# The down product of five blocks in seven products over pairs of inner tiles, with the weights' combinations kept in DRAM

## The chip, the cores and the metric

The kernel runs on one core of one Trainium2 chip. The metric is the device time of one execution in microseconds (us). A core has five engines that run side by side and wait for each other through semaphores: PE (TensorE, matrix products; PEld are its weight loads), DVE (VectorE), ACT (ScalarE), POOL (GpSimd) and SP (SyncE), which issues almost all transfers between DRAM and the on-chip memory SBUF. Matrix products land in PSUM, which has eight banks of 512 float32 columns on 128 partitions.

## What is computed

Two layers, each a Fourier mixing (A) and a gated product (B), on x of 2048 rows and 640 columns:

```python
def _A_ref(x, dft_seq_re, dft_seq_im, dft_hid_re, dft_hid_im):
    a = jnp.einsum("bsd,ed->bse", x, dft_hid_re)
    b = jnp.einsum("bsd,ed->bse", x, dft_hid_im)
    return jnp.einsum("ts,bse->bte", dft_seq_re, a) - jnp.einsum("ts,bse->bte", dft_seq_im, b)

def _B_ref(x, w_gate, w_up, w_down):
    g = jnp.einsum("bsd,df->bsf", x, w_gate)
    u = jnp.einsum("bsd,df->bsf", x, w_up)
    return jnp.einsum("bsf,fd->bsd", _sigmoid(g) * u, w_down)

x = x + _A_ref(_layernorm(x), ...)
x = x + _B_ref(_layernorm(x), ...)
x = x + _A_ref(_layernorm(x), ...)
x = x + _B_ref(_layernorm(x), ...)
```

The inner width F is 1728: 13 tiles of 128 and a tail of 64. Everything is float32, and the kernel keeps that precision by splitting each operand into a high and a low float16 part; one product is then three matmul passes (high x high, high x low, low x high).

## The kernel before

x stays in SBUF (`X`, 16 groups of 128 rows). The Fourier mixing uses the symmetry of the matrices (folded rows), so the kernel also tests that the matrices have it: `load_rows`/`test_rows` and `load_cols`/`test_cols` read parts of the DFT matrices in layer 0 and 1 into two buffers in turn (SP), compare them (DVE, lines 1295 to 1298 and 1312 to 1315) and add the squares (ACT, line 1273). Weights are tested for their size too (`absmax`, line 229). If a test fails, a general path follows; it is not entered with these inputs.

The gated product goes in four blocks of 512 rows per layer (`block[b]`). A block has a gate and up part and a down part.

- Gate and up, block 0 of a layer: `gate_up` takes one inner tile per step, three passes each over five 128-row pieces of x, 512 columns wide (PE line 1047), into two banks per tile. `gated_parts` then splits the result into high and low parts for the down product (lines 1071 and 1072).
- Gate and up, blocks 1 to 3: `seven` takes two inner tiles per double step in a form with seven products of half blocks (PE line 1093, 256 columns wide; the tail tile on line 1176). The weights' combinations for it (`S`, 512 KB per tile) are made in layer 0 and kept in DRAM, and `load_s` brings G, S and U of a tile back for each block. `snap` copies a running sum from PSUM to SBUF (ACT, line 1097), after which the same bank goes on accumulating. `part_three` adds (DVE, 1129 and 1130), `gate` applies the sigmoid (ACT, 1139), `up` multiplies (DVE, 1149 and 1151), `up_parts` splits (ACT 1160, DVE 1161). A double step holds four banks, and the chains of the two tiles before hold two more until `up`.
- Down: `down` has two steps for each of four row groups. It multiplies 13 inner tiles in three passes and the tail in two with both 320-column halves of the weights (PE line 1240), one bank per half, and adds the two banks to `X` (DVE line 1255).

All work is written out in one order by hand. `steps` lists the products; `at(u, f, ...)` puts a job at place u among the steps, so that it is issued before that step's matmuls, and in a double step of `seven` at one of four places. Each engine runs its own instructions strictly in the order of issue, SP's transfers too. While a block's down part runs, the next block is normalised (`pair_stats`, `pair_scale`, `pair_apply`, `pair_combine`, `pair_parts`, DVE, ACT and POOL) and turned round by transposing transfers (`pair_transpose`, SP line 512), and its first weights are loaded.

Memory in SBUF is dealt out by `Slots`: 388 units of 128 float32 columns, of which 218 are fixed. A freed place is taken again by a later tile, whose first writer then waits for the last reader.

At the layer change the last rows of layer 0 are folded (`fold_stats`, `fold_power`, `fold_scale`, `fold_rows`, `fold_join`) while PE works through products of the Fourier mixing (`sequence`, line 771, and `hidden`, line 853). The reciprocal root of the variance (`rstd_power`, `rstd_step`, lines 396 to 407) runs on POOL in small instructions; `fold_scale` adds lines 602 to 607. The first layer's opening has the same work in an order of its own (`OPENING`).

## Time and profile before

| | |
|---|---|
| Time, median of 3 runs | 1177.77 us (1177.05 to 1178.28) |
| The profiled execution: its own time | 1176.77 us |
| its span, first to last instruction | 1174.6 us |
| mean granted TensorE clock | 0.985 |
| PE matmuls in all | 8784 |
| down matmuls (line 1240) | 2624, eight blocks of 328 |
| gate and up part of a block 1 to 3 | 80.5 to 80.8 us |
| down part of a block | 44.5 to 44.6 us |
| DMA moved | 216.41 MB, mean 184 GB/s |

How to read the profile: a group line gives source line, engine, operation, output <- input with partitions x elements and type, count | busy us, mean ns of one | idle time of the engine just before these instructions and what ended it. The chain of waits follows the last instruction back to whatever released it. A line of the view by stretch gives the stretch, its length, then busy us and (count) of PE, PEld, DVE, ACT and POOL, the granted clock, the busy share of the 16 DMA engines, and GB/s. A line in the order of time gives start, length, engine, line and operation; idle time before it stands in brackets with what ended it. "SPq" is SP's queue of transfers: the length is the issue, not the landing.

### The profile page before, as it was taken

To read this page: it belongs to the slowest core of one execution; us is meant where nothing else is said; L and a number is where in the kernel's file an instruction comes from. 1 tells how busy PE (TensorE), PEld (TensorE's weight loads), DVE (VectorE), ACT (ScalarE), POOL (GpSimd) and SP (SyncE) were. 2 spreads that over 40 slices of the span, in tenths; PEclk is the share of its full clock that TensorE was granted. 3 is DMA by queue.
4 is the path that set the end of the run, shared out by engine and by line. 5 is a ranking of instruction groups with operands and counts; after the bars stand their busy time and mean duration, and the time that the engine had idled before them with its cause. 6 is when DMAs were issued, how large, how long until landed. Compare 5 with 4: busy or idle time off the path is not lost.

```text
span 1174.6 us, 22659 instructions
## 1 busy us (share of the span) xinstructions
PE 1135.1 (97%) x8784; PEld 861.1 (73%) x8784; DVE 731.8 (62%) x1571; ACT 503.7 (43%) x1078; POOL 170.5 (15%) x365
## 2 busy tenths in 40 slices
PE   5699999999999999999999999999999999999997
PEld 2367445788878887888776744678887888788874
DVE  8694998768656776676326476746975457524530
ACT  5665475245524653365303422415552455225420
POOL 3414565210102010100011101000000001000000
PEclk9699999999999999999999999999999999999999
DMA  9353797859595969779301642687959773767301
GB/s 277 124 154 95 251 337 269 229 176 261 168 215 168 262 176 225 218 228 251 83 15 58 242 134 62 192 233 227 249 159 241 234 253 94 178 199 255 120 19 38
DMA packets 225622, 216.41 MB, mean 184 GB/s; under 512 B 68034, under 2 KB 181851, under 8 KB 225502
## 3 DMA queue, kind: packets, MB, share of 16 engines
q1 hardware_dynamic: 224862, 212.23, 61.9%
q0 software_dynamic: 640, 2.62, 0.6%
q8 instruction: 71, 1.16, 0.4%
q14 instruction: 49, 0.40, 0.1%
HBM read 171.03 MB, written 30.40 MB: 171 GB/s over the span
## 4 chain that ended last, share of the span: by engine, by line
PE 86%; issue 4%; POOL 3%; DMA 2%; DVE 2%; ACT 2%; SPq 0%; POOLq 0%; DVEq 0%; ACTq 0%
PE acc L1093 36%; PE acc L1240 30%; PE acc L1047 12%; PE acc L771 2%; PE acc L853 2%; PE acc L1176 2%; DMA kept_o<-big 1%; DVE big L238 1%; DMA big<-kept_w 1%; POOL quad L397 0%; DMA big<-in_ct 0%; DVE big L662 0%; SPq L1289 0%; POOL big L998 0%; PE acc L778 0%
## 5 line engine op out<-in xcount | busy, mean ns | idle before, releaser
L1093 PE MATMUL acc<-big 128*128 128x256 f16 x4212 | 462.9, 273 | 0.1
L1093 PEld LDWEIGHTS <-big 128*128 128x128 f16 x4212 | 411.6, 98 | 49.0 <-DMA big<-kept_w 0.4
L1240 PE MATMUL acc<-big 128*128 128x320 f16 x2624 | 357.7, 299 | 0.0
L1240 PEld LDWEIGHTS <-big 128*128 128x128 f16 x2624 | 256.4, 98 | 100.0
L1097 ACT ACTIVATE big<-acc 128x256 f32<-128x256 f32 x312 | 116.5, 381 | 193.8 <-PE acc L1093 189.0
L1047 PE MATMUL acc<-big 128*128 128x512 f16 (+1 forms) x990 | 176.6, 341 | 3.8 <-ACT big L527 1.7
L1047 PEld LDWEIGHTS <-big 128*128 128x128 f16 x990 | 96.3, 98 | 83.3 <-ACT big L236 2.6
L1273 ACT ACTIVATE big<-big 128x768 f32<-128x768 f32 (+8 forms) x104 | 79.5, 764 | 132.5 <-DVE big L1298 96.4
L1161 DVE TENSOR_TENSOR big<-big 128x512 f16<-128x512 f32 x78 | 53.8, 690 | 110.0 <-ACT big L1160 110.0
L1255 DVE SCALAR_TENSOR_TENSOR big<-acc,big 128x320 f32<-128x320 f32 x64 | 28.4, 484 | 82.8 <-PE acc L1240 82.7
L238 DVE SCALAR_TENSOR_TENSOR big<-big 128x640 f16<-128x640 f32 (+6 forms) x81 | 62.9, 815 | 4.7 <-ACT big L236 4.7
L1139 ACT ACTIVATE big<-big 128x512 f32<-128x512 f32 x78 | 47.9, 627 | 38.2 <-DVE big L1130 37.3
L1295 DVE TENSOR_TENSOR big<-big 128x256 f32<-128x256 f32 x64 | 26.7, 416 | 55.5 <-DMA big<-in_ct 55.5
L236 ACT ACTIVATE big<-big 128x640 f16<-128x640 f32 (+6 forms) x81 | 49.7, 665 | 14.3 <-DMA big<-big 8.8
L1130 DVE TENSOR_TENSOR big<-big,acc 128x512 f32<-128x512 f32 x78 | 53.2, 682 | 4.1 <-PE acc L1093 3.9
L771 PE MATMUL acc<-big 128*128 128x256 f16 (+5 forms) x288 | 44.0, 315 | 11.7 <-ACT big L657 9.7
L1149 DVE SCALAR_TENSOR_TENSOR big<-acc,big 128x256 f32<-128x256 f32 x78 | 32.6, 418 | 34.4 <-PE acc L1093 30.1
L1160 ACT ACTIVATE big<-big 128x512 f16<-128x512 f32 x78 | 48.8, 625 | 6.5 <-DVE big L1151 5.6
L771 PEld LDWEIGHTS <-big 128*128 128x128 f16 (+1 forms) x288 | 31.8, 116 | 24.6 <-ACT big L657 12.5
L853 PE MATMUL acc<-big 128*128 128x321 f16 (+3 forms) x324 | 49.2, 304 | 0.0
L505 ACT ACTIVATE big<-big 128x384 f16<-128x384 f32 (+2 forms) x48 | 28.9, 647 | 34.6 <-DVE big L487 22.6
L853 PEld LDWEIGHTS <-big 128*128 128x128 f16 (+3 forms) x324 | 28.8, 96 | 19.2 <-issue 7.5
(169 smaller groups left out, 975.2 us busy)
## 6 DMA issues: line engine op xcount, KB each, us to landing
big<-kept_w SPq DMA_DIRECT2D x125, 320.0 KB
big<-kept_s SPq DMA_DIRECT2D x75, 512.0 KB
big<-in_ct SPq DMA_DIRECT2D x256, 128.0 KB
big<-kept_w SPq DMA_DIRECT2D x78, 192.0 KB
kept_w<-big SPq DMA_DIRECT2D x41, 320.0 KB
big<-in_ct SPq DMA_DIRECT2D x32, 256.0 KB
kept_s<-big SPq DMA_DIRECT2D x13, 512.0 KB
big<-in_wg SPq DMA_DIRECT2D x16, 320.0 KB
```

The costliest lines, as they stand in the source:

```text
L236: nc.scalar.activation(dh, src, AF.Copy, scale=s)
L238: nc.vector.scalar_tensor_tensor(dl, src, s, dh, op0=OP.mult, op1=OP.subtract)
L771: nc.tensor.matmul(o, xv[:, 384 * xp + c0 : 384 * xp + c0 + n], moving(r, cps[cp]), start=(i % 2 == 0 and r == 0 and xp == HI and cp == HI ...
L853: nc.tensor.matmul(ps[:m, :EC], z[:, at : at + m], w[:, 384 * wp : 384 * wp + EC], start=(d == 0 and zp == HI and wp == HI), stop=(d == ND ...
L1047: nc.tensor.matmul(ps, w[wp][:, d * P : (d + 1) * P], xt[:, xp, :], start=(d == 0 and wp == HI and xp == HI), stop=(d == ND - 1 and wp == LO))
L1093: nc.tensor.matmul(ps, wt, xt, start=start and n == 0, stop=n == len(todo) - 1, skip_group_check=not start)
L1097: nc.scalar.activation(dst, ps, AF.Copy)
L1130: nc.vector.tensor_tensor(v, v, other, op=OP.add)
L1160: nc.scalar.activation(s.parts[HI], v, AF.Copy)
L1161: nc.vector.tensor_tensor(s.parts[LO], v, s.parts[HI], op=OP.subtract)
L1240: nc.tensor.matmul(held["pd", e][0][:, :EH], held["ht", j].parts[hp][:, i * P : (i + 1) * P], held["w", 2, j].parts[wp][:, e * EH : (e + 1 ...
L1273: nc.scalar.activation(v, v, AF.Square, accum_out=new_sum()[:p])
```

## The change

Layer 0's block 2 and all four blocks of layer 1 (`PAIRED`) get another down part, `down_pairs`. Twelve inner tiles form six pairs; the rows of a block form two halves of two row groups, the 640 output columns two halves of 320. Each pair's 2 x 2 product of halves is made with seven products in place of eight, and sums over the pairs stay in PSUM: product n over all six pairs is one run of 18 matmuls per row group, 23 where the thirteenth tile and the tail are added (`REST`). Four banks per row group (a to d) are read by DVE twice each into `X`, in part while the bank goes on accumulating: bank a takes products 1, 6, 7 and the leftover 8, and is read after each.

The left sides are made beside the gate and up part: `first_parts`, `second_parts` and `sum_parts` take the place of the plain splits. The right sides are the weights and four combinations of them, T1 to T4. They are made once in layer 0, blocks 1 and 2 (`load_raw`, `make_t`, `split_t`, `keep_t`), kept in DRAM, and T2 to T4 are loaded for each paired block (`load_t`, 18 transfers of 160 KB), T2 and T3 into the place of the block's turned-round rows. The scales DS and PH change with it, and half of the even tiles' weights is tested from a separate load (`load_others`, `test_others`).

In paired blocks G, S and U are loaded separately and later, and `Slots` deals out places in fours below a limit, with the left sides at the top. The matrix tests no longer start between place 12.5 of a block and 4.5 before the next. In layer 1 the joins of hidden groups 2 and 3 move into block 0. `rstd` of the folds and of the first normalisation runs on DVE but for the power itself; a factor 2 is folded in; `fold_join` is issued in three rounds over both halves; evictions at the layer change come one or two places earlier; a folded row is kept in DRAM between blocks 2 and 3.

```diff
-DS = 2.0**11
+DS = 2.0**9
...
-PH = 2.0**-16
+PH = 2.0**-18
...
+NP = 6
+PAIRED = (2,), (0, 1, 2, 3)
...
-    def rstd_step(t, n, to):
+    def rstd_step(t, n, to, on=nc.gpsimd, times=-1.0):
         c = [t[:, :n, k] for k in range(24)]
-        nc.gpsimd.tensor_tensor(c[16], c[14], c[15], op=OP.mult)
...
+        on.tensor_tensor(c[16], c[14], c[15], op=OP.mult)
+        on.tensor_tensor(c[17], c[16], c[15], op=OP.mult)
+        on.tensor_scalar(c[18], c[17], -0.5 * to, 1.5 * to, op0=OP.mult, op1=OP.add)
+        on.tensor_tensor(c[19], c[18], c[15], op=OP.mult)
+        if on is nc.vector:
+            on.scalar_tensor_tensor(c[20], c[12], times, c[19], op0=OP.mult, op1=OP.mult)
...
-    def load_s(j):
-        nc.sync.dma_start(take(5, "G", j).f16, kept["w", 0, j])
...
+    def load_s(j, do="GSU"):
+        if "G" in do:
+            v = take(8, "GU", j).f32
...
+    def gated_parts(j, paired=False):
+        if paired and j < 2 * NP:
+            if j % 2 == 0:
+                first_parts(j // 2, held["hf", j].f32)
+            else:
+                second_parts(j // 2, held["hf", j - 1].f32, held["hf", j].f32)
+                sum_parts(j // 2)
...
+    def first_parts(p, v):
+        a = both(take(6, "A", p, top=UNITS - 8 * NP), 768)[:, :, :256]
+        f = take(8, "af", p).f32
+        nc.vector.tensor_tensor(f[:, 512:768], v[:, :256], v[:, 256:], op=OP.subtract)
+        nc.scalar.activation(a[:, 0], v[:, :256], AF.Copy)
+        nc.vector.tensor_tensor(a[:, 1], v[:, :256], a[:, 0], op=OP.subtract)
+
+    def second_parts(p, v, w):
+        a, f = both(held["A", p], 768)[:, :, 256:], held["af", p].f32
+        s1, s2, s4 = (f[:, 256 * n : 256 * (n + 1)] for n in (0, 1, 3))
+        nc.scalar.activation(a[:, 0], w, AF.Copy)
+        nc.vector.tensor_tensor(s1, v[:, 256:], w[:, 256:], op=OP.add)
+        nc.vector.tensor_tensor(s2, s1, v[:, :256], op=OP.subtract)
+        nc.vector.tensor_tensor(s4, w[:, :256], s2, op=OP.subtract)
+        nc.vector.tensor_tensor(a[:, 1], w, a[:, 0], op=OP.subtract)
+
+    def sum_parts(p):
+        f, s = held["af", p].f32, both(take(8, "AS", p, top=UNITS), 1024)
+        for c in (slice(0, 512), slice(512, 1024)):
+            nc.scalar.activation(s[:, 0, c], f[:, c], AF.Copy)
+        for c in (slice(0, 512), slice(512, 1024)):
+            nc.vector.tensor_tensor(s[:, 1, c], f[:, c], s[:, 0, c], op=OP.subtract)
+        drop("af", p)
...
+    def make_t(p):
+        v, w = (held["dr", 2 * p + k].f32 for k in range(2))
+        b11, b12, b21, b22 = v[:, :EH], v[:, EH:], w[:, :EH], w[:, EH:]
+        nc.vector.tensor_tensor(b11, b12, b11, op=OP.subtract)
+        nc.vector.tensor_tensor(b12, b22, b12, op=OP.subtract)
+        nc.vector.tensor_tensor(b22, b22, b11, op=OP.subtract)
+        nc.vector.tensor_tensor(b21, b21, b22, op=OP.subtract)
...
+    LEFT = {1: ("A", 0), 2: ("A", 1), 4: ("A", 2), 5: ("AS", 0), 6: ("AS", 1), 7: ("AS", 2), 3: ("AS", 3)}
+    CHAIN = {1: "a", 2: "c", 5: "b", 3: "b", 4: "d", 6: "a", 7: "a", 8: "a"}
+    READ = {1: (0, 0), 2: (0, 0), 5: (1, 1), 3: (0, 1), 4: (1, 0), 6: (0, 1), 7: (1, 0), 8: (1, 1)}
+    REST = (2, 3, 4, 8)
...
+    def down_pairs(b, todo, store):
...
+        def mm():
+            for n, i in todo:
+                first = (CHAIN[n], i) not in held
+                if first:
+                    held[CHAIN[n], i] = bank()
+                mms = []
+                for p in range(NP) if n < 8 else ():
+                    a = both(held[LEFT[n][0], p], 256, LEFT[n][1])[:, :, i * P : (i + 1) * P]
...
+                for m, (a, w) in enumerate(mms):
+                    nc.tensor.matmul(held[CHAIN[n], i][0][:, :EH], a, w, start=first and m == 0, stop=m == len(mms) - 1,
+                                     skip_group_check=not first)
...
+        def post():
+            for n, i in todo:
+                ps, k = held[CHAIN[n], i]
...
+                nc.vector.scalar_tensor_tensor(xe, ps[:, :EH], CB, xe, op0=OP.mult, op1=OP.add)
...
+            if b in PAIRED[layer]:
+                if first or b < last:
+                    order = [[(n, 0), (n, 1)] for n in (1, 5, 2, 3, 6, 4, 7, 8)]
+                else:
+                    order = [[(m, i), (n, i)] for i in range(2) for m, n in ((1, 2), (6, 5), (7, 3), (4, 8))]
+                steps += [down_pairs(b, todo, not first) for todo in order]
+                for p in range(NP):
+                    for n, u in ((2, d0 + 0.2), (3, d0 + 0.9), (4, d0 + 2.6)):
+                        at((u if first or b < last or n == 4 else block[b] + 2 + n) + 0.1 * p, load_t, n, b, p)
...
+                    elif q[0] == 0 and j > 3 and b in PAIRED[layer]:
+                        k = j % 2
+                        for what, v in (("G", u - 2 - 0.5 * k), ("S", u - (0.5 if j == NF - 1 else 1 + 0.5 * k)), ("U", u - k)):
+                            at(v, load_s, j, what)
...
-            u0, u1 = block[0] + 8, block[2] + 14
+            free = (block[0] + 8, block[0] + 12.5), (block[1] - 4.5, block[1] + 12.5), (block[2] - 4.5, block[2] + 12.5)
```

More of the change, by code (lines that the diff above doesn't have):

```diff
@@ L681, in spill, with spill_row, load_row @@
             drop(key, i)
+    def spill_row():
+        keep(held["fw"].f16[0:1], "fw")
+        drop("fw")
+    def load_row():
+        nc.sync.dma_start(take(3, "fw").f16[0:1], kept.pop(("fw",)))
     def load_spilled(i):
@@ L1102, in part_one @@
         chain = chain[:, :256]
-        v, w = (take(4, n, j, high=6).f32 for n in ("hv", "hw"))
+        v, w = (take(4, n, j, high=0 if paired else 6).f32 for n in ("hv", "hw"))
         held["step", j] = (chain, kc, other, ko, v, w)
```

290 lines of the change are left out of this document (223 added, 67 removed).

## The prediction

> **What bounds the kernel now.** I read the page first: busy shares, then the shares of the chain that ended last, then the costliest groups.
>
> ```profile
> PE 1135.1 (97%) x8784; PEld 861.1 (73%) x8784; DVE 731.8 (62%) x1571; ACT 503.7 (43%) x1078; POOL 170.5 (15%) x365
> PE 86%; issue 4%; POOL 3%; DMA 2%; DVE 2%; ACT 2%; SPq 0%; POOLq 0%; DVEq 0%; ACTq 0%
> L1240 PE MATMUL acc<-big 128*128 128x320 f16 x2624 | 357.7, 299 | 0.0
> ```
>
> TensorE is busy for 97% of the span, and the line with the down product (L1240) never waits. Next I asked for busy time by stretch (columns: stretch, its length, busy us and count of PE, PEld, DVE, ACT, POOL, clock, DMA share, GB/s).
>
> ```profile
> 0.00:100.00 100.00, 74.91 (x404) 45.73 (x405) 77.98 (x170) 61.25 (x126) 37.71 (x109) 0.86 0.64 191
> 188.00:1121.20 933.20, 929.59 (x7575) 737.45 (x7574) 575.55 (x1281) 383.84 (x848) 84.48 (x208) 1.00 0.66 189
> ```
>
> From 188 us on TensorE stands still for 933.20 - 929.59 = 3.6 us. So a matmul removed there is worth its whole time, as long as no other engine becomes late; the first 100 us hold 25 us of idle TensorE and are set by other engines. Last, the chain of waits in time gives the price of the two products (and of two evictions in a row).
>
> ```profile
> 617.76 0.89 DVE big L1255 x2
> 745.88 44.55 PE acc L1240 x328
> 790.43 71.39 PE acc L1093 x654
> ```
>
> A down matmul takes 44.55 / 328 = 0.1358 us, a 256-wide one of the gate and up product 71.39 / 654 = 0.1092 us.
>
> **The change, part by part.** *Matmuls.* A plain block has 4 row groups x 2 halves x (13 tiles x 3 passes + 2) = 328. A paired block has 6 pairs x 7 products x 2 row groups x 3 passes = 252, and 4 outputs x 2 row groups x 5 = 40 for the two tiles left over: 292. Five blocks lose 36 each: 180 x 0.1358 = 24.4 us, all of it on TensorE, which sets the end. A down product shrinks to 292 x 0.1358 = 39.7 us.
>
> The new form adds up to 23 matmuls in a row to one bank, where the old one alternated between two. The only 320-class matmuls of the trace that stay in a bank are those of L853.
>
> ```profile
> 635.86 16.09 PE L853 MATMUL acc<-big 128*128 128x321 f16 x108
> 90.27 0.25 PEld L853 LDWEIGHTS <-big 64*128 64x128 f16 x3 [0.27 <-issue]
> ```
>
> They take 16.09 / 108 = 0.149 us, 0.013 more. If the bank were the cause, 5 x 292 x 0.013 = 19 us of the gain would go. But that line loads 64-row weights among the 128-row ones, and each such change leaves a 0.27 us hole; L1093 also stays in one bank for 6 to 9 matmuls and has no holes. I take 0 (bounds 0 and +19). The Trainium skill, "TensorE: Matmul & The Clock Gate", section "Wait — 56ns, not 53.3ns?", has start-to-start at columns / 2.4 GHz plus about 2.5 ns whatever the bank. That gives 135.8 ns for 320 columns, which the trace agrees with, and 136.3 for 321, where L853 shows 149; by the rule the gain stays 24.4, by the bare row it would be 5.
>
> *VectorE and ScalarE.* For each pair of inner tiles VectorE forms four combinations of 256 columns and takes the low part of seven pieces of 256 in place of four: five 256-wide instructions and one 512-wide more than now. Each block also has 8 more evictions of 320.
>
> ```profile
> L1161 DVE TENSOR_TENSOR big<-big 128x512 f16<-128x512 f32 x78 | 53.8, 690 | 110.0 <-ACT big L1160 110.0
> L1129 DVE TENSOR_TENSOR big<-big 128x256 f32<-128x256 f32 x78 | 32.6, 418 | 4.0 <-ACT big L1097 4.0
> L1255 DVE SCALAR_TENSOR_TENSOR big<-acc,big 128x320 f32<-128x320 f32 x64 | 28.4, 484 | 82.8 <-PE acc L1240 82.7
> L229 DVE TENSOR_REDUCE wmax<-big 128x1 f32<-128x640 f16 x40 | 31.1, 806 | 0.0
> L1296 DVE TENSOR_TENSOR big<-big 128x256 f32<-128x256 f32 x64 | 27.2, 425 | 15.4 <-DMA big<-in_ct 15.4
> L1298 DVE TENSOR_TENSOR big<-big 128x128 f32<-128x128 f32 x128 | 31.7, 290 | 2.2
> L238 DVE SCALAR_TENSOR_TENSOR big<-big 128x640 f16<-128x640 f32 x41 | 37.3, 936 | 4.7 <-ACT big L236 4.7
> L918 DVE TENSOR_TENSOR big<-big 128x321 f32<-128x321 f32 x24 | 10.6, 487 | 0.0
> L925 DVE TENSOR_TENSOR big<-big 128x642 f32<-128x642 f32 x16 | 13.8, 870 | 0.1
> ```
>
> Per block that is 6 x (5 x 0.418 + 0.690) = 16.7 us in the gate and up part and 8 x 0.484 = 3.9 us in the down part. What this means is read stage by stage (columns as above).
>
> ```profile
> 232.50:313.10 80.60, 80.60 (x740) 72.14 (x739) 57.97 (x142) 41.28 (x99) 10.16 (x29) 1.00 0.71 207
> 313.10:357.70 44.60, 44.60 (x331) 32.09 (x330) 24.77 (x58) 13.09 (x25) 0.00 (x0) 1.00 0.82 199
> 357.70:438.50 80.80, 80.69 (x739) 72.01 (x738) 59.06 (x150) 46.78 (x109) 12.70 (x36) 1.00 0.77 208
> 664.60:745.70 81.10, 81.10 (x437) 42.50 (x435) 53.12 (x103) 20.10 (x39) 6.52 (x18) 1.00 0.37 110
> 790.30:870.80 80.50, 80.50 (x739) 72.06 (x738) 62.01 (x146) 43.06 (x99) 5.30 (x16) 1.00 0.73 210
> 870.80:915.40 44.60, 44.60 (x331) 32.10 (x330) 24.80 (x58) 13.39 (x26) 2.04 (x2) 1.00 0.91 238
> 915.40:996.00 80.60, 80.60 (x741) 72.15 (x739) 48.95 (x122) 42.68 (x100) 5.43 (x16) 1.00 0.62 196
> ```
>
> Layer 0, block 2 (third row): 59.06 + 16.7 + two more row tests (each 2 x 0.425 + 2 x 0.290 = 1.4) = 78.6 of 80.8. Layer 1, block 0 (fourth row): 53.12 + 16.7 + about 14 for two hidden groups' combine, join and add, which move to its steps 4 and 8 (twenty instructions, eight of 0.487, twelve of up to 0.870) = 84 of 81.1. Layer 1, block 1 (fifth row): 62.01 + 16.7 + 2.8 for two tests + 1 for the weight test that it does in another cut - 7 for a hidden group that leaves = 75.5 of 80.5. Means overstate, since neighbours overlap: two evictions in a row take 0.89, not 0.97. With 0.08 off each I get about 75, 79 and 72. Block 2 of layer 1 (last row) comes to 67 and has room.
>
> So VectorE is 90 to 98% busy in three stages. It works in order; behind it stand the evictions, and behind those ScalarE's sigmoids and copies, for which TensorE waits. Some lag is harmless. Block 0 of a layer holds two of eight banks per tile, so three more tiles of 6.2 us may be open. In the other blocks 51 matmuls (5.6 us) lie between an addition at the end of one double step and the copy, queued on ScalarE behind that addition's sigmoid, which TensorE needs in the next. I expect 2 us of stall in each of the three, 6 in all (bounds 0, and the 20 worked out under the rivals). ScalarE gets one copy of 256 and one of 512 more per pair, about 1.1 us, 6.6 a block beside 43 of 80.5: nothing.
>
> Building the combinations in layer 0 costs VectorE 24 x 0.484 + 12 x 0.936 = 23 us, two thirds in block 1's gate and up part and a third in its down part (first two rows), which have 23 and 20 us free: nothing, or up to 3 us if its 36 transfers get in the way.
>
> *The reused bank.* Product 7 and the leftover step 8 share a bank: TensorE waits until VectorE has read the first. Eighteen matmuls of the other row group (2.4 us) cover the 0.484 us read, unless VectorE is held up by test data at that moment.
>
> ```profile
> DVE big L1295 <- DMA big<-in_ct: 13.1, 3, 7.0
> DVE big L1161 <- ACT big L1160: 9.8, 8, 2.2
> SPq L1289 <- ACT big L1273: 18.5, 8, 5.6
> ```
>
> The rows are waits: total, times, longest; VectorE's between 871 and 916 us and between 790 and 871, the sync queue's between 745 and 916. The first shows such waits of up to 7 us in a down part. I take 1 us for all five (bounds 0 and 5 x 4.6 = 23). The Trainium skill, "Perfetto Trace Analysis", section "Matmuls", wants independent groups to rotate through banks, so that an eviction overlaps the next group; this change breaks that at one place per block. By the rule each of the five pays the exposed reads of both row groups, 5 us in all in place of 1; no run here shows it yet.
>
> *DMA and the sync queue.* A paired block loads 18 combinations of 160 KB and stores halves.
>
> ```profile
> 881.30 5.34 SPq L512 DMA_TRANSPOSE big<-big  x2
> 886.70 2.55 SPq L1289 DMA_DIRECT2D big<-in_ct  x4
> 904.44 0.53 SPq L1018 DMA_DIRECT2D big<-kept_w  x1
> ```
>
> 18 x 0.53 = 9.5 us of issue, less 8 test loads of 0.64 moved out, plus four stores: about +6 us, in a down part where four transposes (10.7), 28 test loads (17.9) and 12 weight loads (6.4) already take 35 of 44.6. The queue fills its 39.7 us. The combinations stand first and are used 22 to 33 us later, so what gets late are the tests; that is in the 1 us above.
>
> *The layer change.* The idle time there stands in brackets:
>
> ```profile
> 627.54 0.39 PE L771 MATMUL acc<-big 128*128 128x256 f16 x2 [0.40 <-ACT big L657]
> 628.41 0.28 PE L771 MATMUL acc<-big 128*128 128x256 f16 x1 [0.47 <-DVE big L662]
> 629.98 0.39 PE L771 MATMUL acc<-big 128*128 128x256 f16 x2 [1.28 <-ACT big L657]
> 653.50 0.77 PE L519 MATMUL acc<-ident,big 128*128 128x128 f16 x10 [0.88 <-ACT big L900]
> ```
>
> Behind the first three is a chain from the last down eviction over GpSimd's small instructions; six of them go to VectorE, and the two halves of the join are interleaved. Of the 3.5 us I take 2.5 (bounds 0 and 3.5).
>
> *The opening.* Its chain also runs over GpSimd:
>
> ```profile
> 36.99 1.38 POOL quad L397
> 38.44 0.70 POOL quad L401
> 42.41 0.35 POOL coef L607
> L1378 DVE TENSOR_SCALAR small<-fin 128x1 f32<-128x1 f32 x1 | 0.2, 154 | 0.2 <-POOL fin L1375 0.2
> ```
>
> L401 to L607 take 4.3 us there; on VectorE six instructions of about 0.15 to 0.2 take near 1.2. That is 3 us each time it is on the chain, four times at most; against it VectorE now waits in order for the power (1.38) and is itself 78% busy. I take -3 (bounds -8 and +4).
>
> *Sum.* The profiled execution took 1176.77 us, 2.2 beyond its span: 1176.8 - 24.4 - 2.5 - 3 + 6 + 1 = 1153.9. The median of the runs, 1177.77, is 1.0 above the profiled one, so 1155 is what I expect of the median.
>
> **The rivals.** *All hidden:* VectorE's slack within a block takes up everything: 1148. For it: no TensorE wait in any block today, and full slices of VectorE (11.5 of 12.2 us) that held nothing up. Against it: they stood alone, never for a whole stage.
>
> *VectorE sets three stages:* its busy time plus waits it cannot avoid, of the kind of L1161 behind ScalarE (9.8 us in block 1). Block 0: 79 + about 13 against 81, 11 us; block 1: 72 + 10 against 80.5, 2, and 3 since its new 1920-wide weight test (some 3 x 0.806) comes in one piece; layer 0: 75 + 10 against 80.8, 4. That is 20 in place of 6: 1169.
>
> *Slower: the seven-product weights come late.* In paired blocks S is issued one step ahead, not two; for the odd tile 63 matmuls x 0.1092 = 6.9 us before its use, behind a test load that waits for ScalarE (third row above, up to 5.6 us). Four blocks with six double steps each: the kernel is slower once each loses over (1178 - 1148) / 24 = 1.25 us; at 1.5 us it is 1184. Against it: where VectorE is not late, the queue is ahead.
>
> *The saving isn't there:* long chains in one bank run at L853's 0.149 us: 1155 + 19 = 1174.
>
> **How the numbers follow.** Forecast (1150 to 1160) 0.45, all hidden 0.20, VectorE-set 0.22, late weights 0.09, one-bank chains 0.04. The likeliest gives 1155. The range leaves out the late weights and the one-bank case and a little at either end: 1145 to 1171. A difference under 0.2% (2.4 us) cannot be told from none; 1174 lies near that bound, so I split it: faster 0.88, same 0.03, slower 0.09.
>
> **What would show it.** Right: 292 matmuls per paired down part at 0.136 us; idle TensorE after 188 us below 10 us, most of it in layer 0 block 2 and layer 1 blocks 0 and 1, ended by ScalarE or VectorE; VectorE near 90% there; gaps near 628 us gone. Wrong: TensorE waiting for kept_s or kept_t, holes at steps 7 to 8 of every block, or a down matmul of 0.149 us.

## The result, and the profile after

| | before | after |
|---|---|---|
| Time, median (range) of 4 runs | 1177.83 us (1177.05 to 1178.28) | 1264.68 us (1260.36 to 1270.65) |
| ratio, 95% interval | | 1.0742 (1.0695 to 1.0788) |
| The profiled execution, its span | 1176.77, 1174.6 us | 1270.65, 1268.8 us |
| mean granted clock | 0.985 | 0.954 |

The change costs 87 us where 23 were to be saved. From the page of the kernel after (busy time and instructions of each engine, then groups of instructions with the idle time before them):

```profile
PE 1150.7 (91%) x8604; PEld 858.4 (68%) x8604; DVE 850.3 (67%) x1885; ACT 530.3 (42%) x1150; POOL 155.8 (12%) x289
L1155 PE MATMUL acc<-big 128*128 128x256 f16 x4212 | 495.8, 282 | 54.8 <-ACT big L1159 24.8
L1421 PE MATMUL acc<-big 128*128 128x320 f16 x1460 | 204.3, 302 | 19.0 <-DVE big L1438 14.9
```

All 180 matmuls are gone (8604 against 8784; 1460 = 5 x 292). Idle TensorE rose from 1174.6 - 1135.1 = 39.5 to 1268.8 - 1150.7 = 118.1 us, by 78.6. And TensorE is busy for 15.6 us more although 24.4 us of work left: the rest runs 40.0 us slower. 78.6 + 40.0 - 24.4 = 94.2 us, the whole difference of the spans. In new line numbers L1155 is the product of `seven`, L1421 and L1438 are product and read of `down_pairs`, L1159 is `snap`, L1526 to L1529 and L1504 are a row test's comparisons and square, L1047, L1049 and L1051 load G, S and U.

By stretch (stretch, length, busy us and count of PE, PEld, DVE, ACT, POOL, clock, DMA share, GB/s) the kernel after shows:

```profile
233.40:325.90 92.50, 84.51 (x740) 73.54 (x738) 63.16 (x152) 44.35 (x105) 11.11 (x28) 0.96 0.75 221
370.50:485.10 114.60, 93.07 (x740) 77.17 (x739) 81.47 (x208) 54.14 (x127) 12.27 (x34) 0.88 0.76 207
485.10:531.00 45.90, 41.12 (x295) 29.11 (x293) 28.06 (x64) 13.05 (x24) 0.00 (x0) 0.96 0.87 231
670.60:711.50 40.90, 40.90 (x336) 29.37 (x335) 28.34 (x61) 21.19 (x43) 5.07 (x17) 1.00 0.31 102
711.50:792.60 81.10, 81.10 (x438) 42.57 (x436) 75.14 (x152) 22.61 (x48) 7.20 (x18) 1.00 0.44 138
838.50:936.20 97.70, 87.83 (x739) 74.64 (x738) 73.90 (x182) 48.21 (x117) 6.12 (x17) 0.94 0.76 218
982.50:1072.70 90.20, 84.78 (x739) 73.82 (x738) 65.36 (x164) 48.23 (x117) 7.46 (x17) 0.95 0.64 208
1072.70:1112.40 39.70, 39.70 (x294) 28.57 (x293) 22.97 (x45) 9.92 (x18) 0.00 (x0) 1.00 0.79 189
1112.40:1217.00 104.60, 88.58 (x740) 75.08 (x738) 52.57 (x112) 42.78 (x111) 2.04 (x2) 0.92 0.60 191
```

The rows are: gate and up of layer 0's block 1 (80.6 before) and 2 (80.8); block 2's down part; the layer change (46.9 before); layer 1's block 0 (81.1), 1 (80.5) and 2 (80.6); block 2's down part; gate and up of block 3 (80.7). Six gate and up parts have the form with seven products. These five lose 12, 34, 17, 10 and 24 us, also where VectorE is busy for half of the time (last row); the sixth, layer 0's block 3, loses 5 (80.6 before, 85.5 after). Block 0 of layer 1, where VectorE is busy for 75.14 of 81.10, loses nothing. The layer change before, for comparison:

```profile
617.70:664.60 46.90, 43.39 (x336) 30.21 (x334) 26.75 (x48) 21.35 (x43) 9.67 (x33) 0.96 0.46 160
```

What TensorE waited for (total, times, longest):

```profile
PE acc L1155 <- ACT big L1159: 24.8, 10, 4.5
PE acc L1155 <- DMA big<-kept_s: 17.6, 9, 5.8
PE acc L1421 <- DVE big L1438: 14.9, 3, 5.2
PE acc L1155 <- DMA big<-kept_w: 12.3, 9, 3.3
PE acc L1247 <- DMA big<-kept_w: 9.4, 4, 3.0
```

The last group, L1247, is the tail tile of `seven`. There are three kinds of wait: weights (kept_s, kept_w) 39.3 us, ScalarE's copy 24.8, the reused bank 14.9. The chain of waits in the longest stage, from the kernel after, shows what stands behind the copy:

```profile
379.60 6.24 DMA big<-in_ct
385.94 0.44 DVE big L1527
386.40 0.51 DVE big L1529 x2
386.98 0.13 ACT big L1504
...
387.91 0.28 ACT big L1159
388.23 19.55 PE acc L1155 x154
407.79 6.76 DMA big<-kept_s
414.59 4.62 PE acc L1155 x27
```

A piece of matrix takes 6.24 us to land; VectorE stands at its comparison, ScalarE at the square behind it, and the copy TensorE needs stands behind the square. Then S takes 6.76 us and TensorE waits for that. So the tests' data and the weights come late. A run without an interval is a single one; the four runs of the changed kernel spread over 10 us. The experiments ask whether VectorE's load, the later issue, the scarce places or the tests make them late.

### The profile page after: what moved, and what is told of

Read it like the earlier page. It is cut to its first block, busy times and chain, and to the rows that moved or that the text cites. A ratio compares the mean times of both kernels' runs of the same rounds, so it can differ in the third digit from the quotient of the medians.

```text
span 1268.8 us, 22864 instructions
## 1 busy us (share of the span) xinstructions
PE 1150.7 (91%) x8604; PEld 858.4 (68%) x8604; DVE 850.3 (67%) x1885; ACT 530.3 (42%) x1150; POOL 155.8 (12%) x289
## 3 DMA queue, kind: packets, MB, share of 16 engines
q0 software_dynamic: 640, 2.62, 0.5%
## 4 chain that ended last, share of the span: by engine, by line
PE 56%; DMA 19%; DVE 13%; SPq 4%; ACT 3%; issue 3%; POOL 2%; DVEq 0%; ACTq 0%; POOLq 0%
PE acc L1155 19%; PE acc L1100 12%; PE acc L1421 10%; PE acc L1471 7%; DMA big<-in_ct 6%; DMA big<-kept_w 5%; PE acc L879 4%; PE acc L797 2%; PE acc L1247 2%; SPq L1520 2%; DMA big<-kept_s 2%; DVE big L256 1%; DMA big<-big 1%; DMA kept_o<-big 1%; DMA big<-in_x 1%
## 5 line engine op out<-in xcount | busy, mean ns | idle before, releaser
L1155 PE MATMUL acc<-big 128*128 128x256 f16 x4212 | 495.8, 282 | 54.8 <-ACT big L1159 24.8
L1155 PEld LDWEIGHTS <-big 128*128 128x128 f16 x4212 | 424.9, 101 | 124.1 <-issue 26.6
L1421 PE MATMUL acc<-big 128*128 128x320 f16 x1460 | 204.3, 302 | 19.0 <-DVE big L1438 14.9
L1421 PEld LDWEIGHTS <-big 128*128 128x128 f16 x1460 | 143.9, 99 | 77.7 <-issue 17.5
L1159 ACT ACTIVATE big<-acc 128x256 f32<-128x256 f32 x312 | 111.9, 378 | 187.4 <-PE acc L1155 185.6
L1504 ACT ACTIVATE big<-big 128x768 f32<-128x768 f32 (+8 forms) x104 | 79.6, 765 | 155.5 <-DVE big L1529 111.4
L1471 PE MATMUL acc<-big 128*128 128x320 f16 x984 | 134.2, 299 | 0.0
L1526 DVE TENSOR_TENSOR big<-big 128x256 f32<-128x256 f32 x64 | 26.7, 418 | 84.1 <-DMA big<-in_ct 77.9
L256 DVE SCALAR_TENSOR_TENSOR big<-big 128x640 f16<-128x640 f32 (+6 forms) x93 | 71.1, 799 | 9.1 <-ACT big L254 8.7
L254 ACT ACTIVATE big<-big 128x640 f16<-128x640 f32 (+6 forms) x93 | 58.4, 674 | 34.1 <-DVE big L1348 17.5
L1438 DVE SCALAR_TENSOR_TENSOR big<-acc,big 128x320 f32<-128x320 f32 x80 | 36.8, 486 | 45.8 <-PE acc L1421 45.8
L1319 DVE TENSOR_TENSOR big<-big 128x256 f16<-128x256 f32 x30 | 12.7, 423 | 51.2 <-ACT big L1318 51.2
L797 PEld LDWEIGHTS <-big 128*128 128x128 f16 (+1 forms) x288 | 31.0, 113 | 22.6 <-ACT big L676 11.9
```

The source lines that it names most:

```text
L254: nc.scalar.activation(dh, src, AF.Copy, scale=s)
L256: nc.vector.scalar_tensor_tensor(dl, src, s, dh, op0=OP.mult, op1=OP.subtract)
L797: nc.tensor.matmul(o, xv[:, 384 * xp + c0 : 384 * xp + c0 + n], moving(r, cps[cp]), start=(i % 2 == 0 and r == 0 and xp == HI and cp == HI ...
L1155: nc.tensor.matmul(ps, wt, xt, start=start and n == 0, stop=n == len(todo) - 1, skip_group_check=not start)
L1159: nc.scalar.activation(dst, ps, AF.Copy)
L1421: nc.tensor.matmul(held[CHAIN[n], i][0][:, :EH], a, w, start=first and m == 0, stop=m == len(mms) - 1, skip_group_check=not first)
```

## The experiments

**VectorE's load alone** (e1), on the kernel before:

```diff
-        nc.vector.tensor_tensor(s.parts[LO], v, s.parts[HI], op=OP.subtract)
+        for _ in range(3 if heavy and j < 12 else 1):
+            nc.vector.tensor_tensor(s.parts[LO], v, s.parts[HI], op=OP.subtract)
```

> The kernel before, with VectorE's low-part subtraction of 512 columns (0.690 us) done three times instead of once for tiles 0 to 11 in layer 0 block 2 and layer 1 blocks 1, 2 and 3: 24 x 0.690 = 16.6 us more VectorE work per block, the amount the paired blocks add; no transfer and no place in SBUF changes. Theory V (VectorE's load makes the stalls): those four gate and up parts, 80.5 to 80.8 us before, lengthen by tens of us as in the changed kernel (114.6, 97.7, 90.2 and 104.6 us there), 1240 us or more in all. Theory L (weights and test data arrive late, VectorE's load is harmless): each of the four stays within 3 us of 80.7, 1178 to 1188 us in all.

1194.29 us against 1177.22; the four parts by stretch:

```profile
357.67:441.83 84.16, 80.73 (x738) 72.03 (x737) 70.37 (x162) 43.19 (x105) 13.54 (x36) 1.00 0.67 197
792.17:878.41 86.24, 81.05 (x740) 72.03 (x738) 74.20 (x161) 39.13 (x97) 5.72 (x16) 1.00 0.65 193
923.12:1007.41 84.29, 81.06 (x739) 71.95 (x737) 64.04 (x146) 41.30 (x99) 5.80 (x17) 1.00 0.62 200
1052.13:1138.79 86.66, 82.67 (x740) 72.82 (x737) 53.56 (x100) 39.26 (x101) 0.00 (x0) 0.98 0.51 164
```

The parts lose 3.5 to 6.1 us each: more than the 2 of the prediction and the 3 of theory L, and far from 34. The total lies between the two theories, within neither. It costs as much at 53.56 busy us as at 74.20, so the sum of VectorE's time does not decide. The chain of waits in the last of these parts shows what does:

```profile
1120.99 0.69 DVE big L1162
...
1122.35 0.74 DVE cmax L1364
1123.11 0.50 DVE big L1365
...
1124.01 0.19 ACT big L1275
1124.19 0.54 ACT big L1097 x2
```

A hidden test's comparison (here L1364 and L1365) stands behind the added work (L1162), its square (L1275) behind that on ScalarE, and TensorE's copies (L1097) behind the square: the way of the changed kernel, at a tenth to two fifths of its price. VectorE's load alone is not the main cause.

**The later issue alone** (e7) and **the scarce places** (e12), on the kernel before. e12 adds the occupied pieces to e7. A first form of e7 (e2), with layer 0 block 2 as well and G, S and U each in a place of its own, gave no time: SBUF had no free place of six units for it.

```diff
+                    elif q[0] == 0 and j > 3 and (layer, b) in ((1, 1), (1, 2), (1, 3)):
+                        k = j % 2
+                        for what, v in (("G", u - 2 - 0.5 * k), ("S", u - (0.5 if j == NF - 1 else 1 + 0.5 * k)), ("U", u - k)):
+                            at(v, load_s, j, what)
...
+        for q, n in enumerate([4, 4, 4, 4, 4, 4, 4] if not first else ()):
+            at(block[2] + 0.9 + 0.01 * q, hold, n, q)
```

> The kernel before, with G, S and U of tiles 4 to 12 issued at the places of the changed kernel (S one to one and a half steps ahead, U none to one) in layer 1 blocks 1 to 3; VectorE's work is as before, and the places in SBUF are not limited. Theory L1 (this order alone makes the weights late): each of the three gate and up parts, 80.5 before, takes 88 us or more, 1200 us or more in all. Theory L2 (a load comes late where it has to wait for the last reader of its place): within 3 us of 80.5 each, 1177 to 1186 us.

> The kernel of e7_late_loads (the kernel before with the weights of layer 1 blocks 1 to 3 issued late; those parts took 80.4, 80.4 and 80.8 us), and 28 of the 388 places in SBUF, in seven pieces of four, are kept occupied from the start of layer 1 block 2 to the end: as many as the left sides of a paired block take beyond those of a plain one (84 units against 56). Bytes, tests and VectorE's work are as before. Theory P (scarce places alone make the loads wait for the last readers, and the weights late): blocks 2 and 3 take 85 us or more each, 1185 us or more in all. Theory PD (places alone are harmless as long as the DMA engines are not also loaded with more bytes): within 2 us of 80.5 each, 1175 to 1180 us.

e7: 80.40, 80.40 and 80.75 us, 1175.87 in all. e12: 80.48 and 80.79 us in the two blocks, 1177.69 in all. With the bytes of before neither harms. But e12 makes places only a little scarcer. From layer 1's second down part to the end of block 3's gate and up, the sync queue's waits at loads of G, S and U for the last readers of their places add up to 11.9 us in the kernel before, 17.9 in e12, and 99.4 in e13 below, which has the paired blocks and no tests. In e13 those gate and up parts still take 80.4 to 80.6 us. So it is e13 that shows long waits for places to be harmless while the tests' bytes are absent.

**Without the matrix tests** (e3), on the changed kernel:

```diff
-        for q, (load, test, key) in enumerate(tests):
+        for q, (load, test, key) in enumerate(()):
```

> The changed kernel without the symmetry tests of the sequence matrices (their 288 loads, VectorE's comparisons and ScalarE's squares are left out in both layers; the tests of the hidden matrices and of the weights stay). Theory T (test data is late, VectorE and ScalarE wait for it in order, and with them the copies TensorE needs): layer 0 blocks 1 to 3 and layer 1 blocks 1 and 2 come back to within 4 us of 80.7, a gain of some 70 us, while layer 1 block 3, which holds none of these tests, stays near 104. Theory L2 (places): the weights of the paired blocks still wait for the last reader of their place, layer 0 block 2 and layer 1 blocks 1 to 3 stay 8 us or more above 80.7, and the gain is below 50. Theory V: VectorE is relieved by some 20 us per block, so nearly all stalls go, except that layer 1 block 3, where VectorE is busy for 53 of 105 us, is not explained by it.

1178.50 us, 86 less. Gate and up of layer 0 block 2, its down part, gate and up of layer 1 blocks 1 and 3:

```profile
358.10:442.30 84.20, 82.24 (x739) 72.82 (x738) 58.94 (x137) 41.40 (x95) 12.45 (x34) 0.98 0.49 156
442.30:482.19 39.89, 39.89 (x296) 28.72 (x294) 22.16 (x44) 8.50 (x14) 0.00 (x0) 1.00 0.88 247
778.54:858.94 80.40, 80.40 (x739) 72.06 (x737) 55.71 (x122) 37.60 (x87) 6.90 (x17) 1.00 0.50 163
1019.13:1124.76 105.63, 88.37 (x739) 74.86 (x737) 52.79 (x113) 43.27 (x111) 2.04 (x2) 0.92 0.58 190
```

As theory T said, blocks come back to 80.4 and block 3 of layer 1 stays. The wait at the reused bank is gone too, 39.89 us in this down part and those of layer 1's first three blocks: VectorE's waiting for test data had made it. (In e5 and e6 below, with only the comparisons or only the transfers, these down parts take 39.9 us too, so it needs both.) In layer 1's first three blocks the paired work and its 18 loads per block do fit.

**The tests' halves**: work without transfers (e5), transfers without work (e6).

```diff
 e5
-            at(u, load, *key)
+        for k in range(2 if first else 0):
+            at(spots[0] - 1, zero_room, k)
 e6
-            at(v, test, *key)
-            at(v + 0.7 * (w - v), square_rest)
```

> The changed kernel with the tests' comparisons and squares kept at their places, but on two buffers set to zero once: the 288 loads of matrix parts are left out. Theory T1 (what stalls TensorE is the test data's way: VectorE waits for it in order, and ScalarE's copies behind it): nearly as without the tests, 1178 to 1195 us, layer 0 block 2 below 92. Theory T2 (VectorE's and ScalarE's time for the tests, about 1.4 and 1.7 us each, on top of the paired work): 1220 us or more, layer 0 block 2 above 100.

> The changed kernel with the tests' loads kept, without the comparisons and squares that read them. Theory T1a (the tests' 36 MB on the sync queue and the DMA engines make the weights late by themselves): 1220 us or more. Theory T1b (the weights are early enough, and only the wait of VectorE and ScalarE for test data counts): 1178 to 1195 us; layer 1 block 3 near 104 in both, since it has other reasons.

e5 1188.85 us, e6 1228.03 us. So the comparisons alone cost 10.4 us over e3, the transfers alone 49.5, and 26.3 of the 86.2 come only with both. In e6 VectorE and ScalarE do none of this work and wait for none of these loads, yet layer 0 block 2 is 105.47 us, and TensorE waits for weights:

```profile
PE acc L1155 <- DMA big<-kept_w: 35.5, 15, 6.4
PE acc L1155 <- DMA big<-kept_s: 13.6, 7, 6.3
PE acc L1247 <- DMA big<-kept_w: 4.6, 2, 2.6
```

Layer 0 block 1 stays at 93.29 us in e6 (81.70 in e3): there the building of the combinations meets the tests' transfers (without the building, e4 below, it is 82.98).

**Another queue for the test loads**: e9 is the whole change, e14 is e6, both with these loads issued by GpSimd.

```diff
-            nc.sync.dma_start(v[:, g], bass.AP(ct.tensor, (r * S + row) * S, [[P, NS], [d * S, 16], [1, P]]))
+            nc.gpsimd.dma_start(v[:, g], bass.AP(ct.tensor, (r * S + row) * S, [[P, NS], [d * S, 16], [1, P]]))
```

> The changed kernel whole, but the 288 loads of the matrix tests are issued by GpSimd instead of the sync queue; the same bytes move at about the same time, and the sync queue holds the weights, combinations, transposes and stores alone. Theory S (the one in-order queue: a test load that waits for its buffer, or a weight load that waits for its place, keeps what stands behind it): the weights come as in the kernel whose tests moved nothing (1188.9 us), 1185 to 1205 us. Theory D (the DMA engines are full: the transfers themselves are slow while 1.5 to 2 MB of tests and weights per step are under way): nothing is gained by another queue, 1245 us or more.

> The kernel of e6_test_loads_only (tests' loads kept, comparisons and squares left out: 1228.0 us, TensorE waits 54 us for kept_w and kept_s), with these loads issued by GpSimd, so that the sync queue carries none of them. Theory S (the place in the sync queue): the weights come as without any tests, 1178 to 1195 us, TensorE waits below 25 us for weights. Theory D (the share of the DMA engines): 1215 us or more, 45 us of such waits or more.

e9 took 1272.04 us, nothing gained; e14 took 1217.23 us, just inside theory D's range, 11 of e6's 49.5 gained. In e14 TensorE still waits:

```profile
PE acc L1155 <- DMA big<-kept_w: 26.5, 12, 4.9
PE acc L1155 <- DMA big<-kept_s: 16.4, 8, 4.4
...
PE acc L1247 <- DMA big<-kept_w: 6.2, 2, 3.3
```

That is 49.1 us after 53.7, with no test load of the sequence matrices in the sync queue. So the bytes keep the weights late without it. How small the queue's own part is stays inexact: the 11 us are a balance of 8.9 and 7.0 us gained in layer 0's blocks 2 and 3 and 6.2 lost in layer 1's block 1. The move also changes the transfers: over the stages from 186 us on GpSimd is busy for 281 us in place of 80, and the page of e14 counts 44.60 MB as software_dynamic in place of 2.62. The Trainium skill, "DMA: Bandwidth & Descriptors", section "Issuing engines are not separate DMA queues", says that transfers started by different engines end on the same 16 DMA engines and interleave; these two runs agree, with 49.1 us of waits left of 53.7 in e14 and nothing gained in e9. The worst stretch says the same: in layer 0 block 2 the share times the length was 0.77 x 80.8 = 62 us of DMA time before and is 0.76 x 114.6 = 87 after, more than a part of 80.8 us holds. Only there, though: in the other four parts the product is 58 to 74 us, so this sum alone does not explain the 10 to 24 us that they lose.

**Where the tests stand**: e10 undoes the pauses. e4 leaves out pairs and combinations, and keeps the pauses and the rest of the change.

```diff
 e10
-            free = (block[1] + 6, block[1] + 12.5), (block[2] - 4.5, block[2] + 12.5), (block[3] - 4.5, block[3] + 13)
+            free = ((block[1] + 6, block[3] + 13),)
 e4
-PAIRED = (2,), (0, 1, 2, 3)
+PAIRED = (), ()
```

> The changed kernel with the matrix tests spread evenly over the places they had before (51 and 50 steps of a layer), without the pauses, in which the same 74 tests share 41 and 38.5 steps. Theory N (the pauses press too many loads into the gate and up parts): the gate and up parts of layer 0 blocks 1 and 2 and of layer 1 block 1 shorten by 5 us or more each, and the first halves of the down parts pay at most 2 us each, 1230 to 1250 us. Theory M (the tests are harmful wherever they stand in a block without free places): within 10 us of 1264.7.

> The changed kernel with no paired block and without building the combinations: what is left is the layer change and the opening in another order, the limit and the fours in which places are dealt out, the later first loads and the tests' new pauses. If these are harmless: 1177.8 less the 6.0 us measured at the layer change, 1170 to 1174, all gate and up parts 80.5 to 81. If the rounding of places to fours costs something by itself: layer 0 block 1, which is 12 us longer in the changed kernel though it is not paired, stays above 85, and 1178 to 1190 in all.

(There are 84 tests, 42 a layer; 74 is a miscount.) e10 took 1260.42 us, which is in theory M's range. As theory N says, the gate and up parts of layer 0 block 2 and layer 1 block 1 shorten by 8.5 and 12.7 us (layer 0's block 1 only by 1.9), but the down part behind the first, second row, pays it back:

```profile
366.80:472.94 106.14, 87.87 (x739) 74.57 (x739) 78.67 (x197) 53.16 (x125) 13.72 (x34) 0.92 0.82 235
472.94:526.49 53.55, 41.30 (x295) 29.21 (x293) 31.43 (x76) 14.70 (x28) 0.00 (x0) 0.88 0.84 220
```

The down part is 53.55 us where 39.9 is the work: 12 us between steps 7 and 8, not the 2 expected. Over the kernel TensorE waits 37.6 us there, in four places, where the changed kernel has 14.9 in three. e4 took 1183.24 us, a ratio of 1.0047 (1.0029 to 1.0065): even unpaired, layer 0 block 2 is 89.97 us. The total is in the range for places in fours, but its sign is missing: layer 0 block 1 takes 82.98 us, not more than 85. The pauses are needed for the reused bank and press the tests together elsewhere. e4 does not separate them from the new dealing of places.

**The last block** holds no matrix tests. e8 is e3 with the direct stores six steps later, e13 leaves out the hidden tests as well.

```diff
 e8
-                    store_x(b, g, slice(e * EH, (e + 1) * EH))
+                    if b < NB - 1:
+                        late_x.append((b, g, slice(e * EH, (e + 1) * EH)))
...
+                if not first and b < last:
+                    at(len(steps) + 6, store_late)
 e13
-            for load, test, key, u, later in tests:
+            for load, test, key, u, later in ():
```

> The changed kernel without the matrix tests (as in e3_no_tests, 1178.5 us), and the direct stores of paired blocks 0 to 2 of layer 1 are issued six steps into the next gate and up part. Theory Q (the sync queue stands 7.7 and 6.3 us in front of two such stores, which wait for the store by GpSimd before them, and the weights are issued behind): layer 1 block 3 goes from 105.6 to 93 to 97 us, since the waits of 3.5 and 3.2 us for kept_w and the lower clock behind them go; 1166 to 1171 us in all. Theory P (the loads there wait for the readers of their places, whatever the queue does): layer 1 block 3 stays above 102, 1175 us or more.

> The kernel of e8_no_tests_stores_later (1171.0 us, layer 1 block 3 at 98.5) without the tests of the hidden matrices too (14 loads, comparisons and squares in layer 1's blocks 2 and 3 left out). Theory H (these loads wait for ScalarE or VectorE in front of the last block's weights): layer 1 block 3 falls to 82 to 88 us, 1155 to 1161 us in all. Theory P (the weights wait for the readers of their places, and T2 and T3 of the last block, twelve loads in its gate and up part, stand in front of them): it stays above 93 us, 1165 us or more.

In e3 the sync queue waits there like this (total, times, longest), first at the direct stores, then at a load of S whose place is still read, last at hidden loads (L1589):

```profile
SPq L399 <- DMA out<-big,rows: 14.0, 2, 7.7
SPq L1049 <- DVE big L1191: 11.9, 2, 6.2
SPq L1589 <- ACT big L1159: 8.8, 2, 6.4
```

e8: 98.46 us in this part, between the two theories (93 to 97, or above 102), and 1170.97 in all, at the edge of theory Q's range. TensorE's waits left in this part, 12.6 us, are all for weights, while the sync queue stands 18.3 us at hidden loads that wait for ScalarE. e13, the same part and the page's first row:

```profile
1016.38:1097.00 80.62, 80.59 (x739) 71.91 (x737) 42.96 (x96) 37.02 (x87) 0.96 (x1) 1.00 0.48 159
```

```profile
PE 1107.1 (97%) x8604; PEld 841.8 (73%) x8604; DVE 735.1 (64%) x1529; ACT 456.7 (40%) x952; POOL 157.5 (14%) x289
```

1148.88 us against 1177.40. It goes theory H's way and beyond its range: 80.62 us, hardly a wait left. In this part the place of the stores made 7.2 us and the hidden tests 17.8. e13 takes out the hidden tests' loads and work together, so that their place in the sync queue does it is argued from the waits of e8 and not shown apart. e13 leaves every test of the matrices out, so it is a measurement and no version to use.

**All tests, elsewhere** (e15, e16), with the stores of e8:

```diff
+        parts = ((block[1] + 6, block[1] + 12.5, 5), (block[2] + 0.5, block[2] + 12.5, 7), (block[3] + 0.5, block[3] + 13, 14), (d0 + 0.2, d0 + 5.8, 16)) if first else ((block[0] + 8, block[0] + 12.5, 5), (block[1] + 0.5, block[1] + 12.5, 9), (block[2] + 0.5, block[2] + 12.5, 14), (block[3] + 0.5, block[3] + 12.5, 14))
...
+        spots = [u + (v - u) * q / n for u, v, n in parts for q in range(n)]
```

> The whole change with every test, the direct stores of layer 1 six steps later as in e8, and the tests at other places: none in layer 0 block 2, 22 of layer 0's 42 in the last down part of that layer (VectorE 10.8 us, DMA 0.06 busy there), 12 of layer 1's 42 in its last gate and up part, none in a down part with a reused bank, and the tests of the hidden matrices in the last down part (DMA 0.14). Theory R (the tests only harm where VectorE and the DMA engines have no room): layer 0 block 2 falls from 114.6 to 82 to 88 us, the down parts to 39.9, layer 1 block 1 to about 90, 1170 to 1195 us in all. Theory M (the shortage of places makes any test harmful): 1220 us or more.

> The whole change with every test, the direct stores of layer 1 six steps later, and the 84 matrix tests placed by room: of layer 0's 42 now 5 in block 1, 7 in block 2, 14 in block 3 and 16 in its down part; of layer 1's 5, 9, 14 and 14 in the gate and up parts of its four blocks; none in a down part with a reused bank; the hidden tests at the very end of layer 1. Theory R (tests only harm where VectorE and the DMA engines have no room, and at the reused bank): down parts of 39.9 us, layer 0 block 2 below 95, layer 1 blocks 1 to 3 below 95 each, 1175 to 1195 us in all. Theory M (the shortage of places makes any test harmful): 1220 us or more.

In e15 the general path ran behind (the three largest of its lines keep TensorE busy for 2579 us), so the total of 4319.65 us says nothing of the placing. By the edit some hidden loads fall on the same place as the comparison of their buffer; that this set the general path off is likely and not shown. e16 took 1239.58 us, a ratio of 1.0513 (1.0479 to 1.0547). The total is in theory M's range, but part by part theory R's forecasts hold (layer 0 block 2 91.0 us, layer 1 blocks 1 to 3 84.0, 90.6 and 86.3, four down parts 39.89). The time is lost where the tests went: layer 0's block 3 with the sequence products behind it takes 101.5 us (89.9 before), and the last down part, with the hidden tests, 74.7 (44.6 in the changed kernel). Layer 0's last down part took 16 tests at 44.71 us, its length before, which speaks against theory M; the layer change and block 0 behind it took some 8 us more than in e13. So e16 found no room for all the tests beside the pairs; other placings weren't tried.

**The layer change alone** (e11), on the kernel before:

```diff
-                        at(v + 4.4, fold_scale, b, k, k + 1)
+                        at(v + 4.4, fold_scale, b, k, k + 1, nc.vector)
...
-                    at(end + 2.3, fold_join, b)
+                    run(end + 2.3, [(fold_join, b, ALL, (n,)) for n in range(3)])
```

> The kernel before with nothing of the change but the last block's folds and the layer change: the small steps of the reciprocal root there on VectorE, the doubled factor folded in, the join in three rounds over both halves, the earlier evictions. Theory: the 6.0 us by which the layer change shortened are its own, 1170.5 to 1173 us. Rival: they come from what the other edits moved out of the layer change (the fourth block's test spacing, the row kept in DRAM), and 1175 to 1178 us are left.

```profile
619.26:660.20 40.94, 40.94 (x337) 29.43 (x335) 28.40 (x62) 21.43 (x43) 5.07 (x17) 1.00 0.53 181
```

1168.70 us, a ratio of 0.9914 (0.9887 to 0.9940); the stretch is the layer change, 46.9 before. So the 6.0 us are its own, as the theory said, though the total is faster than its range. The ratio says 10 us; the profiled spans differ by 6.8: 6.0 at the layer change, 2.2 behind the last down part, 1.1 in the opening, less 2.5 in layer 0. The rest lies between runs: the kernel before took 1178.95 us in the median beside e11 and 1176.77 in its profile. This is the version to keep: 0.9% faster than the kernel before, with an interval clear of 1.

## Why the prediction was wrong

- *Matmuls, right.* 292 per paired down part and 180 fewer in all; 39.70 / 292 = 0.136 us each in the down part without a wait. The one-bank case fell. The Trainium skill's page "TensorE: Matmul & The Clock Gate" (section "Wait — 56ns, not 53.3ns?") gives the interval by columns and clock, 135.8 ns here, and this agrees; the page does not speak of banks, so that the bank makes no difference is what these 0.136 us show.
- *DMA and the sync queue, the step that failed:* "what gets late are the tests; that is in the 1 us above". It priced issue time only, where its own sum, 35 + 6 = 41 us for a part of 39.7, was already over, and it took late test data for harmless. The tests cost 86.2 us in the changed kernel (e3), of which their transfers alone make 49.5 (e6). Where it allowed 1 us, TensorE waited 39.3 us for weights and 24.8 for ScalarE's copies; without the tests 20.4 and nothing are left (e3), and with their comparisons but no late data 1.1 for the copies (e5). No sum of DMA time per stage was made; 0.77 x 80.8 = 62 us stood in the rows quoted. The sign that it named for being wrong, TensorE waiting for kept_s, came (17.6 us).
- *VectorE, mis-sized twice.* Its added time alone costs 3.5 to 6.1 us a block (e1), not 2. Yet with the tests gone the paired blocks 1 and 2 of layer 1 have no stall (e13), so load alone sets no stage there. The forecast for block 0 of layer 1 was 84 busy us, 79 after the correction, and 2 us of stall; it was 75.1 and none. Busy time was weighed without asking how late the data is for which VectorE waits in order.
- *The reused bank:* 14.9 us in three places, inside the bounds (0 and 23), not 1. The wait was foreseen in kind (VectorE held by test data); with evenly spread tests it is 12 us a block (e10), without tests nothing. The rule of the Trainium skill's page "Perfetto Trace Analysis" (section "Matmuls"), worked out to 5 us in all, came out too small here (14.9) and too large in e3 (no wait), where the covering matmuls were enough.
- *Building the combinations:* "nothing, or up to 3 us". Layer 0 block 1 lost 12 us, 1 of it left in e3.
- *Layer change:* 6.0 us, above the bound of 3.5. The bound summed idle time; the matmuls behind the holes ran slower as well (43.39 busy us before, 40.90 after, for as many).
- *Opening:* no gain of 3 us (188.0 against 188.9).
- *The rivals.* "The seven-product weights come late" was the nearest, at a chance of 0.09 and 1.25 to 1.5 us a double step. Its mechanism was half right: the weights are late beside the test loads, but mostly also when these stand in another queue (e14), and late in the last block too, behind stores and, it seems, hidden loads (e8, e13). "All hidden", 1148, is met by e13's 1148.9, but partly by luck: that kernel has no tests, and its layer change gives 6 us, not 2.5. The kernel before without tests wasn't run; after 188 us its TensorE stands still for only 3.6 us, so little of e13's gain of 28.5 us can come from there.

Not settled: how much of e6's 49.5 us needs the scarce places as well as the bytes. Late issue harmed nothing with the bytes of before (e7), and long waits for places harmed nothing without the tests (e13); the paired blocks with more places, or with the test loads at half their size, weren't tried.

## What to carry to other kernels

Before adding work to a stage, add up each shared resource for that stage alone, the DMA engines too (busy share times length), and look at what is already waiting in order there. Here 62 of 81 us did no harm, and 87 went with the largest loss. The sum is a warning and no forecast: parts of 58 to 74 us lost 10 to 24 us, and a down part at a share of 0.88 lost nothing (e3); the share can pass 1.00, as rows below show, so it is no strict measure of room. A late load for a low-priority check reaches TensorE through every engine that works in order and takes part in the check. Moving such loads to another issuing engine frees the queue, not the bytes.

## What the runs showed of the hardware

A wait of TensorE costs its length, and more behind it. The stretches around the waits that end at 378.54, 388.23 and 414.59 us in the kernel after:

```profile
371.83:374.62 2.79, 2.79 (x24) 2.36 (x25) 2.12 (x5) 2.19 (x4) 0.00 (x0) 1.00 1.05 326
378.54:383.74 5.20, 5.20 (x24) 3.48 (x24) 0.12 (x1) 0.22 (x1) 0.00 (x0) 0.52 1.08 312
388.23:392.23 4.00, 4.00 (x19) 2.82 (x19) 3.31 (x11) 1.98 (x6) 0.00 (x0) 0.50 0.64 189
394.23:396.00 1.77, 1.77 (x19) 1.59 (x17) 1.74 (x6) 0.29 (x1) 0.45 (x2) 1.00 0.70 204
414.59:417.00 2.41, 2.41 (x12) 1.73 (x13) 2.29 (x7) 0.91 (x2) 0.00 (x0) 0.50 1.16 218
```

After 3.92 us of waiting the granted clock is 0.52, and 24 matmuls take 5.20 us instead of 2.79; after the next wait, 4.49 us, it is 0.50, and 1.00 again 6 us later. A wait of 2.87 us (last row) halves it too, one of 2.40 us before 460.43 does not. Over the kernel the same 8604 matmuls take 1150.7 us here and 1107.1 in e13: 43.6 us of slower matmuls beside 78.1 us more of waiting. The Trainium skill, "TensorE: Matmul & The Clock Gate", section "Part 1: The HAM clock gate", has the clock halved after an idle window of about 3.4 us and full after as long a busy one, and these rows agree that waits of 3.92 and 4.49 us halve it; but 2.87 us was enough as well, and the way back took 5 to 6 us of work after the second wait. Here the rows decide: 3.4 us is no safe limit for a wait in this kernel. None of the prediction's stalls had this second half in its price.
